# Fused causal attention and soft MoE: the sums of the last 128 queries added by VectorE, and a start without round trips for two pairs

## The chip, the cores and the metric

The kernel runs on 1 core of one Trainium2 chip. The metric is the device time of one execution in microseconds. The profile records one execution; its span is a little shorter than its time, and every row quoted below counts from the span's start.

## What is computed

Eight batches of eight heads, 576 tokens, head size 64. Each head has a causal attention whose scores get a bias from running sums `cum` of `max(s, 0)`; the output of all heads of a batch goes through a soft mixture of experts.

```python
scores = scale * np.matmul(q, k.transpose(0, 1, 3, 2))
s_pos = np.maximum(s, 0.0)
cum = np.cumsum(s_pos, axis=-1)
bias = -(cum[:, :, :, None] - cum[:, :, None, :])
scores = np.where(causal, -1000000000.0, scores + np.minimum(bias, 0.0))
scores = scores - np.max(scores, axis=-1, keepdims=True)
attn = np.exp(scores)
attn = attn / (np.sum(attn, axis=-1, keepdims=True) + 1e-09)
attn_out = np.matmul(attn, v)
...
logits = x @ phi
d = softmax(logits, axis=0)
slot_input = d.T @ x
slot_out[e] = np.maximum(slot_input[e] @ w1[e], 0.0) @ w2[e]
out = softmax(logits, axis=1) @ slot_out
```

## The kernel before

Two heads make a **pair** and lie in the two halves of the partitions; there are 32 pairs, four to a batch. For the pair p the kernel works in two passes over the scores.

The first pass finds the maximum of every query's row. `mxp` (L370) makes the scores with the queries in the partitions, in four groups `mx.p.0` to `mx.p.3`; groups 0 and 1 are the last 128 queries against keys 0 to 287 and 288 to 575, groups 2 and 3 the other queries. For each piece TensorE does a matmul of queries and keys (`w`) and a second one that adds the key's running sum: its stationary operand `ones2` holds ones in every 32nd row, its moving operand `g` the sums, split into a high and a low fp32r part. VectorE takes the maxima in `red` (L381): for group 0 a plain reduction (L389), for the others a custom operation (L392) that also adds the causal `mask` and is followed by a read of its accumulator.

Then the maxima go into the row form that the second pass needs: `f0` splits them on GpSimd (L403, L404), `f1` transposes them on TensorE (`mt`, L411), `f2` copies them on ScalarE (`hl`, L417), and `md` sends them by a DMA into rows of `g` (L424, L427). The sums come into other rows of `g` by the DMA `cum` (L357, L360). The second pass `sc` (L436) makes the scores again with the keys in the partitions, as three products of high and low parts plus one product from `g` that adds sum and maximum; ScalarE exponentiates (`ex`, L456), GpSimd cuts the causal corner (`cut`, L463) and adds up for the denominators (`zs`, L484 to L490), TensorE multiplies with v (`y`, L533).

A string `ORDER` lists all steps (`mx.16.0`, `f0.16`, `cut.15.0`, ...) and each engine executes its own in that order; SyncE issues nearly all DMAs from one queue. `busy.n` are n matmuls whose results nobody reads. The four expert weight arrays come in 64 blocks of 512 KB: some go early into `pre` (NPRE blocks), the rest into buffers that the attention no longer needs (`get`), the last ones into blocks that the first expert layer has read. The end of the program (from `sit`, L847) is the two expert layers and the output.

```python
groups = [[(0, 4, 0, 288)], [(0, 4, 288, 576)], [(0, 3, 0, 448), (448, 0, 0, 64)],
          [(0, 2, 0, 320), (320, 1, 0, 192)]]
for l, t, k in ((w[:, q0 - 128:q0], w, WK), (ones2, gt, KO)):
    for a, r in enumerate(half):
        nc.tensor.matmul(ps[a][:, d:d + hi - lo], l[r], t[r, k + lo:k + hi],
                         start=t is w, stop=t is gt)
```

## Time and profile before

| what | value |
|---|---|
| median of 3 runs | 415.88 us (414.97 to 416.27) |
| the profiled execution's time | 415.59 us |
| its span | 413.9 us |
| TensorE (PE) busy | 395.3 us, 96% |
| VectorE (DVE) busy | 284.0 us, 69% |
| GpSimd (POOL) busy | 274.8 us, 66% |
| ScalarE (ACT) busy | 239.6 us, 58% |

The profiled execution took 0.29 us less than the median. A share of the whole span mixes three stages: a start of some 21 us, the pairs until about 345 us, and the experts with the output. Each has its own limit, so the views are read by stage.

### The profile page before, as it was taken

The page shows a single profiled execution, that of the slowest core. Times are in us where ns is not written, and L with a number is a line of the kernel's source. Part 1 is how long each engine was busy: PE and PEld are TensorE (multiplying, and loading weights), DVE is VectorE, ACT ScalarE, POOL GpSimd, SP SyncE. Part 2 cuts the span into 40 slices and gives each one's busy share as a digit, 9 for nine tenths or more (in the row PEclk, how much of TensorE's full clock was granted, in tenths as well). Part 3 has the DMA queues.
Part 4 walks back from the last instruction along what each step waited for, and adds up shares of the span by engine and source line. Part 5 has one row for each costly group of instructions (what it writes and reads, how often), then busy time and mean ns, then how long its engine had stood idle before and what let it go on. Part 6 is the DMA issues. An engine that isn't in the chain of part 4 may idle for free.

```text
span 413.9 us, 14533 instructions
## 1 busy us (share of the span) xinstructions
PE 395.3 (96%) x5699; PEld 295.3 (71%) x5699; DVE 284.0 (69%) x952; ACT 239.6 (58%) x717; POOL 274.8 (66%) x376
## 2 busy tenths in 40 slices
PE   8999999999999999999999999999999999999950
PEld 8778777777787777777777787778777777435540
DVE  8956887877877787778767877787778547212460
ACT  3156766586768665866586768666865663220350
POOL 7069899888878888888788878887888740000000
PEclk9999999999999999999999999999999999999995
DMA  3424578526754475447644754463236789999998
GB/s 130 133 80 140 181 260 261 171 89 202 231 172 144 146 232 172 141 148 216 188 142 144 229 176 144 146 193 110 92 89 191 250 234 401 390 412 384 306 329 295
DMA packets 35252, 83.76 MB, mean 202 GB/s; under 512 B 4976, under 2 KB 14192, under 8 KB 35184
## 3 DMA queue, kind: packets, MB, share of 16 engines
q1 hardware_dynamic: 35168, 82.83, 60.6%
q8 instruction: 45, 0.74, 0.7%
q14 instruction: 23, 0.19, 0.1%
q10 hardware_dynamic: 16, 0.01, 0.0%
HBM read 72.43 MB, written 10.03 MB: 199 GB/s over the span
## 4 chain that ended last, share of the span: by engine, by line
PE 81%; DMA 4%; DVE 3%; ACT 2%; issue 2%; SPq 0%; DVEq 0%
PE s L445 25%; PE y L533 19%; PE mx L378 11%; PE sum L562 4%; PE m L1023 3%; PE m L995 3%; DMA g<-hl 3%; PE nat L601 3%; PE lt L666 2%; PE sl L786 2%; PE mt L411 1%; PE po L1061 1%; ACT arena L456 1%; PE x L522 1%; DVE arena L392 1%
## 5 line engine op out<-in xcount | busy, mean ns | idle before, releaser
L456 ACT ACTIVATE arena<-s 128x288 f32<-128x288 f32 (+4 forms) x384 | 114.9, 407 | 31.7 <-PE s L445 30.6
L445 PE MATMUL s<-w 64*128 64x288 f32 (+4 forms) x1152 | 109.2, 304 | 0.3 <-DVE nmin L743 0.2
L533 PE MATMUL y<-arena 128*64 128x512 f32 (+4 forms) x640 | 90.8, 427 | 0.0
L445 PEld LDWEIGHTS s<-w 64*128 64x128 f32 (+1 forms) x1152 | 81.9, 177 | 10.2 <-ACT arena L456 1.2
L463 POOL TENSOR_SCALAR_AFFINE_SELECT arena<-arena 128x256 f32<-128x256 f32 (+1 forms) x160 | 63.7, 411 | 23.6 <-ACT arena L456 22.0
L484 POOL TENSOR_TENSOR arena<-arena 128x896 f32<-128x896 f32 x31 | 69.3, 2237 | 8.7 <-PE mt L411 5.9
L533 PEld LDWEIGHTS y<-arena 128*64 128x64 f32 x640 | 42.5, 137 | 44.8 <-issue 34.1
L392 DVE CUSTOM_DVE_ANT_0 arena<-mx,arena 128x448 bf16<-128x448 f32 (+3 forms) x128 | 59.0, 461 | 17.6 <-PE mx L378 15.8
L378 PE MATMUL mx<-w 64*128 64x288 f32 (+4 forms) x384 | 56.6, 302 | 0.9 <-ACT w L341 0.9
L445 PE MATMUL s<-g 64*128 64x288 f32 (+4 forms) x384 | 56.5, 291 | 0.5 <-DMA g<-hl 0.5
L392 DVE CUSTOM_DVE_ANT_0 junk<-mx,arena 64x64 bf16<-64x64 f32 (+3 forms) x128 | 49.2, 385 | 10.4 <-PE mx L378 8.7
L378 PE MATMUL mx<-g,ones 64*128 64x288 f32 (+4 forms) x384 | 53.1, 300 | 0.0
L347 DVE TENSOR_TENSOR w<-arena,w 128x576 fp32r<-128x576 f32 x64 | 50.6, 810 | 0.2
L486 POOL TENSOR_TENSOR arena<-arena 128x640 f32<-128x640 f32 x31 | 48.3, 1557 | 2.4
L341 ACT CAST w<-arena 128x576 fp32r<-128x576 f32 x64 | 40.4, 677 | 13.7 <-DMA arena<-in_qk_dram 12.7
L545 ACT COPY arena<-y 128x512 f32<-128x512 f32 x32 | 18.8, 589 | 48.8 <-PE y L533 48.8
L389 DVE TENSOR_REDUCE mx<-mx 128x1 f32<-128x288 f32 x64 | 26.7, 447 | 27.5 <-PE mx L378 23.3
L378 PEld LDWEIGHTS mx<-w 64*128 64x128 f32 x384 | 38.5, 185 | 3.2 <-ACT w L341 1.0
L378 PEld LDWEIGHTS mx<-g,ones 64*128 64x128 f32 x384 | 38.2, 185 | 0.3
L445 PEld LDWEIGHTS s<-g 64*128 64x128 f32 (+1 forms) x384 | 35.1, 177 | 1.5 <-DMA g<-hl 1.0
L488 POOL TENSOR_TENSOR arena<-arena 128x384 f32<-128x384 f32 x31 | 31.8, 1026 | 2.4
L403 POOL TENSOR_SCALAR mh<-mx 128x10 fp32r<-128x10 f32 x32 | 20.1, 627 | 17.5 <-DVE mx L392 17.1
(168 smaller groups left out, 573.6 us busy)
## 6 DMA issues: line engine op xcount, KB each, us to landing
arena<-in_qk_dram SPq DMA_DIRECT2D x32, 576.0 KB
pre<-in_w_dram SPq DMA_DIRECT2D x36, 512.0 KB
arena<-in_v_dram SPq DMA_DIRECT2D x32, 320.0 KB
arena<-in_w_dram SPq DMA_DIRECT2D x19, 512.0 KB
arena<-rs SPq DMA_DIRECT2D x60, 144.0 KB
out_dram<-pre SPq DMA_DIRECT2D x20, 256.0 KB
ww<-in_w_dram SPq DMA_DIRECT2D x6, 512.0 KB
out_dram<-ww SPq DMA_DIRECT2D x8, 256.0 KB
```

Of the source, the lines that this page charges most:

```text
L341: nc.scalar.copy(w[:, o:o + S], st["raw", p][:, i, :])
L347: nc.vector.tensor_tensor(w[:, o + 2 * S:o + 3 * S], st["raw", p][:, i, :], w[:, o:o + S].bitcast(F32), op=ALU.subtract)
L378: nc.tensor.matmul(ps[a][:, d:d + hi - lo], l[r], t[r, k + lo:k + hi], start=t is w, stop=t is gt)
L389: nc.vector.tensor_reduce(m[:, a, c:c + 1], ps[:, d:d + w], axis=AX.X, op=ALU.max)
L392: nc.vector.tensor_tensor_reduce(out=junk()[r, 0:w], in0=ps[r, d:d + w], in1=mask[r, o:o + w], scale=1.0, scalar=m[:, a, 4:5] if i == 1 el ...
L445: nc.tensor.matmul(ps[a][0:n, d:d + hi - lo], t[r, ko + 128 * j:ko + 128 * j + n], t[r, qo + lo:qo + hi], start=x == 0, stop=x == 3)
L456: nc.scalar.activation(st["p", p][0:n, a, o + lo:o + hi], ps[0:n, d:d + hi - lo], AF.Exp, bias=0.0, scale=0.125)
L463: nc.gpsimd.affine_select(d, d, pattern=[[0, 2], [1, n]], compare_op=ALU.is_ge, fill=0.0, base=0, channel_multiplier=-1)
L484: eng.tensor_tensor(z[:, :, 128:576], pt[:, :, 128:576], pt[:, :, 576:1024], op=ALU.add)
L486: eng.tensor_tensor(z[:, :, 256:576], z[:, :, 256:576], pt[:, :, 1024:1344], op=ALU.add)
L488: eng.tensor_tensor(z[:, :, 384:576], z[:, :, 384:576], pt[:, :, 1344:1536], op=ALU.add)
L533: nc.tensor.matmul(y[r, lo - 64:512], vt[:, j, r], st["p", p][:, g, OFF[j] + lo - 128 * j:OFF[j] + 576 - 128 * j], start=(j == 0), stop=(j ...
```

## The change

For the pairs from 2 on, groups 0 and 1 lose the second matmul. In its place a DMA `cb` sends the pair's running sums (576 KB) from a new DRAM copy `cumf` to all 128 partitions, GpSimd's `cm` sets the causal corner of that tile to a large negative number, and VectorE's custom operation adds the tile while it searches the maximum. Two such tiles take 2304 words of each partition, and NPRE goes from 24 to 21.

For the pairs 0 and 1 the sums are added on TensorE straight from the fp32 tile `cum`, with a column of the identity as stationary operand; their maxima get into rows of `g` by 20 matmuls with a mostly zero operand `turn` and two copies on ScalarE, with no DMA. Their `low` parts move from VectorE to GpSimd, and some clearing of buffers moves from the start into a step `clear` on GpSimd after `f0.0`. Of the 46 `busy` matmuls of the start 9 are left. The sums now lie in partitions 0 to 31 and 64 to 95.

```diff
-NPRE = 24
+NPRE = 21
...
-    nc.sync.dma_start(out=s_sb, in_=s)
+    nc.sync.dma_start(out=s_sb[0:NP], in_=s[0:NP])
+    nc.scalar.dma_start(out=s_sb[64:64 + NP], in_=s[NP:NH])
...
+    op(("clear",), clear)
+    op(("ch", 0), lambda: nc.scalar.copy(cumhl[:, 0, :].bitcast(F32R), cum))
+    op(("ch", 1), lambda: nc.gpsimd.tensor_tensor(cumhl[:, 1, :].bitcast(F32R), cum, cumhl[:, 0, :], op=ALU.subtract), [("ch", 0)])
...
-            nc.vector.tensor_tensor(w[:, o + 2 * S:o + 3 * S], st["raw", p][:, i, :],
+            (nc.gpsimd if p < 2 else nc.vector).tensor_tensor(w[:, o + 2 * S:o + 3 * S], st["raw", p][:, i, :],
...
-                for l, t, k in ((w[:, q0 - 128:q0], w, WK), (ones2, gt, KO)):
+                for l, t, k in ((w[:, q0 - 128:q0], w, WK), (ones2, gt, KO) if p > 1 else (None, cum, 0))[:1 if p > 1 and c == 4 else 2]:
...
-                        nc.tensor.matmul(ps[a][:, d:d + hi - lo], l[r], t[r, k + lo:k + hi],
-                                         start=t is w, stop=t is gt)
+                        x = ident[r, 64 * a + p:64 * a + p + 1].broadcast_to([64, 128]) if l is None else l[r]
+                        nc.tensor.matmul(ps[a][:, d:d + hi - lo], x, t[r, k + lo:k + hi],
+                                         start=t is w, stop=t is not w or p > 1 and c == 4)
...
+                if c == 4 and p > 1:
+                    nc.vector.tensor_tensor_reduce(
+                        out=junk()[:, 0:w], in0=ps[:, d:d + w], in1=reg("cb", p % 2).rearrange("p (a x) -> p a x", a=2)[:, a, lo:hi], scale=1.0,
+                        scalar=m[:, a, 4:5] if i else NEG, op0=ALU.add, op1=ALU.max, accum_out=m[:, a, 4:5])
+                    continue
...
+        def cb():
+            nc.sync.dma_start(out=reg("cb", p % 2), in_=cumf[p:p + 1].broadcast_to([128, 2 * S]))
+
+        def cm():
+            d = reg("cb", p % 2).rearrange("p (a x) -> p a x", a=2)[:, :, S - 128:S]
+            nc.gpsimd.affine_select(d, d, pattern=[[0, 2], [-1, 128]], compare_op=ALU.is_ge, fill=NEG,
+                                    base=0, channel_multiplier=1)
...
+                for c in range(NCH):
+                    for k in range(4):
+                        nc.tensor.matmul(st["mt", p][c // 4][32 * k:32 * k + 32, 128 * (c % 4):128 * (c % 4) + 128],
+                                         turn[:, c, k, :], ident, start=True, stop=True)
...
+                nc.scalar.copy(gt[:, 0:512], st["mt", p][0])
...
+                nc.scalar.copy(gt[:, 512:KO], st["mt", p][1][:, 0:KO - 512])
...
-    op(("cw",), lambda: nc.sync.dma_start(out=cumd, in_=cumhl), [("cum", 1)])
+    def copy_full():
+        for a in range(2):
+            nc.sync.dma_start(out=cumf[:, S * a:S * a + S], in_=cum[64 * a:64 * a + NP])
```

`ORDER` is written anew as a whole. On TensorE in the middle of the program, at the start of pair 16's first pass (`mx_16`; `w` are its keys and queries, `g` and `ones` the sums), these rows stood before:

```order
L445 MATMUL s_1_0_3042<-g_96 128x288
L445 MATMUL s_1_1_3043<-g_96 128x288
L378 MATMUL mx_16_0_3065<-w_101 128x288
L378 MATMUL mx_16_1_3066<-w_101 128x288
L378 MATMUL mx_16_0_3065<-g_98,ones_109 128x288
L378 MATMUL mx_16_1_3066<-g_98,ones_109 128x288
L666 MATMUL lt_3072<-arena 32x128 x4
```

and these now:

```order
L493 MATMUL s_1_0_3057<-g_99 128x288
L493 MATMUL s_1_1_3058<-g_99 128x288
L398 MATMUL mx_16_0_3080<-w_104 128x288
L398 MATMUL mx_16_1_3081<-w_104 128x288
L714 MATMUL lt_3088<-arena 32x128 x4
```

The two matmuls with the sums are gone, and what surrounds them kept its order.

On GpSimd at the same place the last additions for pair 13's denominators (L490, now L538), the split `mh` of pair 15's maxima, and the cuts of pair 14 stood so before:

```order
L490 TENSOR_TENSOR arena<-arena 64x2x64
L403 TENSOR_SCALAR mh_3024<-mx_115 128x2x5
L404 TENSOR_TENSOR mh_3024<-mx_115,mh_3024 128x2x5
L463 AFFINE_SELECT arena<-arena 128x2x128 x3
L463 AFFINE_SELECT arena<-arena 64x2x64
```

and now, with `cm` of pair 16 as L430:

```order
L538 TENSOR_TENSOR arena<-arena 64x2x64
L444 TENSOR_SCALAR mh_3052<-mx_119 128x2x5
L445 TENSOR_TENSOR mh_3052<-mx_119,mh_3052 128x2x5
L430 AFFINE_SELECT arena<-arena 128x2x128
L511 AFFINE_SELECT arena<-arena 128x2x128 x3
L511 AFFINE_SELECT arena<-arena 64x2x64
```

`cm` stands behind the split and ahead of the next pair's cuts here; for the pairs 17 and 18 it stands ahead of the split.

On SyncE's DMA queue where a batch ends, from the DMA `md` of pair 13 (first L424 row) to that of pair 14, with the reciprocal denominators `rs` sent to all partitions, weights (`pre`), v and the next queries and keys between them, it was:

```order
L424 DMA g_98<-hl_2740 4x5x128
L357 DMA g_97<-cumd 4x576
L571 DMA arena<-rs_0_2724 64x576 x4
L860 DMA pre<-in_w_dram 128x1024
L506 DMA arena<-in_v_dram 128x640
L331 DMA arena<-in_qk_dram 128x1152
L571 DMA arena<-rs_0_2724 64x576 x2
L424 DMA g_96<-hl_2916 4x5x128
```

and it is now:

```order
L476 DMA g_101<-hl_2755 4x5x128
L426 DMA arena<-cumf 128x1152
L376 DMA g_100<-cumd 4x1x576
L619 DMA arena<-rs_0_2738 64x576 x4
L908 DMA pre<-in_w_dram 128x1024
L554 DMA arena<-in_v_dram 128x640
L350 DMA arena<-in_qk_dram 128x1152
L619 DMA arena<-rs_0_2738 64x576 x2
L476 DMA g_99<-hl_2931 4x5x128
```

One more transfer of 576 KB, `cb` (L426), has come in ahead of all that stands between the two.

## Rows read from the trace of the kernel before

**Rows 1.** The page, busy time of each engine: us, share of span, instructions.
```profile
PE 395.3 (96%) x5699; PEld 295.3 (71%) x5699; DVE 284.0 (69%) x952; ACT 239.6 (58%) x717; POOL 274.8 (66%) x376
```
**Rows 2.** Busy time in stretches: us, PE PEld DVE ACT POOL, PEclk, DMA share, GB/s.
```profile
280.00:320.00 40.00, 40.00 (x617) 31.27 (x614) 30.57 (x107) 26.33 (x83) 33.34 (x45) 1.00 0.38 119
360.00:380.00 20.00, 19.82 (x249) 8.86 (x241) 3.55 (x6) 2.39 (x4) 0.00 (x0) 1.00 1.03 410
```
**Rows 3.** Timeline of PE, first pass of pair 0: start us, us, what.
```profile
10.88 0.29 PE L378 MATMUL mx<-g,ones 64*128 64x288 f32 x2
11.02 0.29 PE L378 MATMUL mx<-w 64*128 64x288 f32 x2
11.15 0.30 PE L378 MATMUL mx<-g,ones 64*128 64x288 f32 x2
11.29 0.36 PE L378 MATMUL mx<-w 64*128 64x448 f32 x2
```
**Rows 4.** Chain of waits, in order: start us, us; matmuls sl end a batch.
```profile
100.35 0.86 PE sl L786 x8
...
141.43 0.86 PE sl L786 x8
...
152.00 6.41 DMA g<-hl
...
182.97 0.86 PE sl L786 x8
...
193.54 6.54 DMA g<-hl
...
224.63 0.86 PE sl L786 x8
```
**Rows 5.** Timeline of DVE, first maxima of pair 0.
```profile
11.25 0.82 DVE L389 TENSOR_REDUCE mx<-mx 128x1 f32<-128x288 f32 x2 [0.56 <-PE mx L378]
11.99 0.51 DVE L392 CUSTOM_DVE_ANT_0 arena<-mx,arena,mx 128x288 bf16<-128x288 f32 x1
12.42 0.08 DVE L392 DVE_READ_ACCUMULATOR2_ANT mx<- 128x1 f32 x1
```
**Rows 6.** Groups by line: busy us, mean ns | idle before, releaser.
```profile
L463 POOL TENSOR_SCALAR_AFFINE_SELECT arena<-arena 128x256 f32<-128x256 f32 (+1 forms) x160 | 63.7, 411 | 23.6 <-ACT arena L456 22.0
L488 POOL TENSOR_TENSOR arena<-arena 128x384 f32<-128x384 f32 x31 | 31.8, 1026 | 2.4
L562 PE MATMUL sum<-arena,onesl 128*32 128x72 f32 x1024 | 22.5, 228 | 0.0
```
**Rows 7.** Timeline of POOL and of PE around the split of a pair's maxima.
```profile
149.10 0.54 POOL L404 TENSOR_TENSOR mh<-mx,mh 128x10 fp32r<-128x10 f32 x1
...
151.41 0.28 PE L411 MATMUL mt<-ident,mh 128*20 128x128 f32 x1
```
**Rows 8.** Busy time in stretches of a batch's end, columns as in Rows 2.
```profile
144.00:146.00 2.00, 2.00 (x18) 1.14 (x18) 1.97 (x10) 1.43 (x3) 1.54 (x2) 1.00 0.09 24
...
154.00:156.00 2.00, 2.00 (x14) 1.00 (x14) 1.94 (x11) 1.43 (x3) 1.92 (x3) 1.00 0.91 222
```
**Rows 9.** Timeline of the start: casts, scan, first matmul, filler, split, first scores.
```profile
4.50 1.67 DVE L268 TENSOR_TENSOR_SCAN arena<-arena 64x576 f32<-64x576 f32 x1
5.38 1.25 ACT L341 CAST w<-arena 128x576 fp32r<-128x576 f32 x2 [3.31 <-DMA arena<-in_qk_dram]
10.64 0.40 PE L378 MATMUL mx<-w 64*128 64x288 f32 x2
13.45 2.27 PE L937 MATMUL busy<-ident 128*128 128x128 f32 x18
16.49 0.20 POOL L404 TENSOR_TENSOR mh<-mx,mh 128x10 fp32r<-128x10 f32 x1
21.22 0.68 PE L445 MATMUL s<-w 64*128 64x288 f32 x6
```
**Rows 10.** Timeline of SyncE's queue at the end: first output transfers.
```profile
383.09 15.54 SPq L1067 DMA_DIRECT2D out_dram<-pre  x20
```

More of the change, by code (lines that the diff above doesn't have):

```diff
@@ new lines @@
+e1.7.1.0 ex.31.2.1 cut.31.0 ex.31.3.0 get.11 a.30.1 cut.31.3 zc.31 cut.31.2 a.30.2 z.31.0 ax.31 a.30.3 a.30.4 rb.30
+ev.30 get.14 z.31.1 get.15 evx.31 t6.6 get.13 a.31.0 nr.29 z.31.2 a.31.1 z.31.3 nr.28 sm.31 a.31.2 e1.7.2.0 a.31.3
+nr.30 a.31.4 rb.31 ev.31 get.16 get.18 get.17 lt.28 nr.31 lt.29 lt.30 get.22 lt.31 get.20 t7.6 c0.7 t2.7 t3.7 busy.1
+m.0 nat.31 t8.6 nat.28 m.1 nat.29 natd.31 natd.28 m.2 natd.29 nat.30 m.3 t4.7 nat0.7 m.4 natd.30 c1.7 get.23 natd0.7
+t5.7 m.5 get.24 t6.7 busy.2 m.6 t7.7 m.7 s0.7 s1.7 ct t8.7 get.28 get.21 get.19 get.12 sit.0 get.26 get.27 get.25
@@ L164 @@
+sit.1 s2.7 s2p.7
 """
@@ L316, in every32, with clear @@
         return t.bitcast(F32).rearrange("(a r) x -> a r x", r=32)[:, i, :]
+    def clear():
+        for t in gs[2:]:
+            nc.gpsimd.memset(t[:, KO:].bitcast(F32), -1.0)
+            ones_rows(t)
+        nc.gpsimd.memset(onesl, 0.0)
+        nc.gpsimd.memset(onesl[:, 4 * HP - 1:4 * HP], 1.0)
+        nc.gpsimd.memset(dn[64:128, 1, :], 0.0)
+        nc.gpsimd.memset(reg("x", 0)[64:128, 0:DM], 0.0)
+        for i in range(NPB):
+            nc.gpsimd.memset(reg("p", i).rearrange("p (a x) -> p a x", a=2)[64:128, :, 1536:1600], 0.0)
+        nc.gpsimd.memset(acc, 0.0)
+    op(("clear",), clear)
+    op(("ch", 0), lambda: nc.scalar.copy(cumhl[:, 0, :].bitcast(F32R), cum))
+    op(("ch", 1), lambda: nc.gpsimd.tensor_tensor(cumhl[:, 1, :].bitcast(F32R), cum, cumhl[:, 0, :], op=ALU.subtract), [("ch", 0)])
     def scores(p):
@@ L408, in f1 @@
         def f1():
+            if p < 2:
+                st["mt", p] = [bank(f"mt{i}") for i in range(2)]
+                for c in range(NCH):
+                    for k in range(4):
+                        nc.tensor.matmul(st["mt", p][c // 4][32 * k:32 * k + 32, 128 * (c % 4):128 * (c % 4) + 128],
+                                         turn[:, c, k, :], ident, start=True, stop=True)
+                return
             mh = st.pop(("mh", p))
@@ L421, in md @@
         def md():
-            hl = st.pop(("hl", p))
-            if p:
-                nc.sync.dma_start(out=every32(gt, 1)[:, 0:KO].rearrange("l (c q) -> l c q", c=NCH), in_=hl.bitcast(F32))
+            if p < 2:
+                nc.scalar.copy(gt[:, 512:KO], st["mt", p][1][:, 0:KO - 512])
                 return
-            for a in range(2):
-                (nc.scalar if a and p == 0 else nc.sync).dma_start(out=every32(gt, 1)[2 * a:2 * a + 2, 0:KO].rearrange("l (c q) -> l c q", c=NCH),
-                                  in_=hl[2 * NCH * a:2 * NCH * (a + 1)].bitcast(F32))
+            nc.sync.dma_start(out=every32(gt, 1)[:, 0:KO].rearrange("l (c q) -> l c q", c=NCH), in_=st.pop(("hl", p)).bitcast(F32))
         op(("md", p), md, [("f2", p)])
@@ L492, in scores @@
         g = old(NZ)
-        op(("zc", p), zc, [("cut", p, 0), dep("sm", g)])
+        op(("zc", p), zc, [("cut", p, 0), dep("sm", g), ("clear",) if p == 0 else None])
         for i in range(4):
@@ L874, in tile_attn_softmoe, with copy_cum @@
     op(("cst",), (fetch, g4, cst[:, 0:128]), [("load", 3)])
-    op(("cw",), lambda: nc.sync.dma_start(out=cumd, in_=cumhl), [("cum", 1)])
+    def copy_cum():
+        for a in range(2):
+            nc.sync.dma_start(out=cumd[a], in_=cumhl[64 * a:64 * a + NP])
+    def copy_full():
+        for a in range(2):
+            nc.sync.dma_start(out=cumf[:, S * a:S * a + S], in_=cum[64 * a:64 * a + NP])
+    op(("cf",), copy_full, [("ch", 0)])
+    op(("cw",), copy_cum, [("cum", 1)])
     op(("phi",), load_phi, [("load", 2)])
@@ L924, in tile_attn_softmoe @@
         op(("pre", i), (get, pre[:, 1024 * i:1024 * (i + 1)]), [("load", min(4 + i, NP - 1))])
[L925 removed]
+    room.sort(key=lambda r: max([0 if x[0] in ("low", "red") else 1 if x[0] == "s" else 3 if x[0] == "t7" else 2 for x in r[1]]))
     last = None
```

353 lines of the change are left out of this document (180 added, 173 removed).

## The prediction

> **What bounds the kernel now.** I read the page's busy times first, then the stretches, the timeline of TensorE, the chain of waits, and last the start and the end. TensorE is busy 96% of the span, far ahead of DVE, POOL and ACT [rows 1]. A busy record alone doesn't show that an engine is at its limit, because matmuls overlap; so see two more things. In the stretch from 280 to 320 us TensorE has no idle time at all, while POOL has 33.3 and DVE 30.6 of 40 us [rows 2]. And a pair of 288-column matmuls (one for each head) starts 0.13 to 0.14 us after the one ahead of it, though its record lasts 0.29 [rows 3]: 288 columns in 0.135 us are 2.1 columns a nanosecond, near the upper of the clock's two levels, and the granted clock of the stretch is 1.00. So in the middle of the program time goes as TensorE's columns go. The chain of waits repeats itself with 41.08 us for a batch of four pairs (100.35 to 141.43). Two batches take 41.54 and 41.66, and in each of them the chain holds a DMA `g<-hl`, the `md`, for 6.4 to 6.5 us [rows 4]: where a batch ends, the queue is so full that the maxima arrive about half a microsecond late. That is the weak place of this kernel.
>
> **The sums of the last queries, pairs 2 to 31.** Each pair loses two steps of 288 columns (both heads run side by side), so 2 x 0.135 = 0.27 us of TensorE, and 30 x 0.27 = **8.1 us**. This lies on the path that sets the end wherever TensorE has no idle time.
>
> On DVE two plain reductions (0.82 us for both) become two custom operations, which follow each other at 0.43 us with the accumulator's read inside [rows 5]: 30 x 0.04 us, hidden, as DVE has 9 us of idle time in 40 [rows 2]. The operand is now fp32 and not bf16. No row shows this form; a custom operation of 288 columns already goes at some 0.67 columns a nanosecond, and if the wider operand doubled its time, the four of a pair would cost 1.7 us more, still under the 2.3 us that DVE idles for each pair. I take nothing.
>
> On POOL `cm` is one more corner cut of 128 x 256 elements, 0.41 us [rows 6], 1.6 us in a batch: 33.3 becomes about 35.9 of 40 us (the same work in a shorter stretch, plus 1.6). That is close. Where it would bite is the split of the maxima: at a batch's end POOL ends it at 149.64 and TensorE transposes at 151.41 [rows 7], so 1.77 us are left, against 0.41 for `cm` and 0.27 for the earlier TensorE. I take nothing for it; behind it the cuts come late next.
>
> **The transfer of the sums.** `cb` brings 0.59 MB a pair. At the rate of the weight loads, 410 GB/s, it takes 1.4 us of the DMA engines; at that of the stretch in which the `rs` rows go to all partitions, 222 GB/s at a share of 0.91, it takes 2.4 us [rows 2, 8]. Nearest is the latter, since this is such a transfer too. In most pairs it falls into idle queues (a share of 0.38 from 280 to 320). At a batch's end it stands ahead of the four and two `rs` transfers, weights, v, queries and keys that are ahead of `md`. Some of it fills the gap before (a share of 0.09 from 144 to 146), the rest makes `md` later. Lower bound: nothing, if it all goes into that gap. Upper bound: 2.4 us at each of the seven batch ends, 16.8 us. I take half a microsecond, which is what a late `md` costs in the two batches that show one, at five of the seven, an estimate that leaves two ends the room that most of them have now: **+2.5 us**. Bounds of the range: 0 and 7 (1 us at all seven).
>
> **The start.** Before, the first matmul waits for the sums' round trip and starts at 10.64, though the casts end at 6.63 and the scan at 6.17 [rows 9]; now it may start at 6.7. From there the first scores start, before, at 21.22, held by the `md` of pair 0. DVE took some 4.8 us for pair 0's maxima (from 11.25 [rows 5] to just ahead of the split, whose second half is at 16.49); with two reductions of pair 1 now between them, 0.8, and a first matmul's results at about 7.5 it is done at 13.1. POOL has five operations of 576 elements ahead of the split, which by 1.03 us for 384 take 1.5 each [rows 6]: 7.7 us from the casts' end, 14.3. Then come the split (0.5, two rows like that at 16.49), 20 matmuls of 128 columns, and two ScalarE copies of 640 columns together (0.7 by the casts). By the `sum` matmuls, which take 32 columns of the array too, 22.5 us for 32 pairs of 16 x 72 columns, the 2560 columns take 1.6 us [rows 6]; by the filler, 0.25 us each (two records to a matmul), 5 us [rows 9]. The former is the nearer shape. That gives 14.3 + 0.5 + 1.6 + 0.7 = 17.1, and with 0.9 for the handovers between four engines (an estimate) 18.0: 3.2 us earlier. TensorE has then about 0.7 us less of pairs 1 and 2 done than before at 21.22, by the five steps of rows 3's kind that it lacks. The fp32 sums of the two pairs cost 1600 columns each at 0.25 us for 128, 3.1 us a pair; that lies beside the waits for DVE and POOL, where 46 filler matmuls ran. If they ran longer than those waits, they would be what is late next. I take **-2.5 us**, with the bounds -4 and +1 (`clear` stands on POOL between the two splits and may delay pair 1).
>
> **The end.** With NPRE down by 3 and 2304 more words of buffers (two blocks of 1024), one block less can be loaded before the experts, and one more is refilled among them. The DMA engines are full from 360 to 380 (share 1.03) [rows 2], and the output starts at 383.09 behind them [rows 10]. A block is 0.52 MB, 1.3 us at 410 GB/s; between 0 and 1.3 I take **+0.7 us**.
>
> **The sum.** -8.1 + 2.5 - 2.5 + 0.7 = -7.4 us, against the profiled execution's 415.59: **408.2 us**, 1.8% below the median of 415.88. A measurement of this kernel tells 0.3%, 1.25 us, from no change.
>
> **The rivals.** *Everything hides.* `cb` fits into idle queues, and the start gains its bound: 415.6 - 8.1 - 4 = 403.5. For it: 38% share in the quiet stretch. Against: the chain already shows `md` late twice.
>
> *The batch ends give it back.* `md` comes 1.3 us later at all seven: 415.6 - 8.1 - 2.5 + 9.1 + 0.7 = 414.8, no change that can be told.
>
> *Slower.* The same mechanism at its upper bound: `cb` pushes the whole 2.4 us in front of `md` at seven batch ends, +16.8: 422.5. It decides from 1.6 us a batch end on, where the waits eat 8.1 + 2.5 - 0.7 and 1.25 more. Against it: the gap at 144 to 146.
>
> *TensorE is not what bounds.* Then the columns removed buy nothing between 40 and 340 us, and 415.6 - 2.5 + 2.5 + 0.7 = 416.3 remains, no change. The pitch in rows 3 speaks against it. The Trainium skill (Perfetto Trace Analysis, Identifying the Most-Contended Engine) has a rule for this rival: matmul busy time says little about how near TensorE is to its limit, and the busy share of the weight loads says more. By that rule the 71% of PEld [rows 1] leave room, and the time would be this rival's 416.3; the trace answers with start-to-start times and not with busy time, so I give the rule's case little.
>
> **How the numbers follow.** The forecast has 0.65, everything hides 0.17, batch ends give it back 0.07, slower 0.07, TensorE not the bound 0.04. The first two are faster by over 0.3%: 0.82; the third and last are within it: 0.11; slower 0.07. The range runs from 403.0, just under the second case, to 413.6, where the forecast's terms stand at +7 for the batch ends and -1 for the start (415.6 - 8.1 - 1 + 7 = 413.5); what is left out is 0.18.
>
> **What would show it.** Right: no `g,ones` matmuls for groups 0 and 1, and a batch of four pairs in the chain at about 40.0 us, 40.5 where `md` is late; first scores near 18 us; POOL near 36 of 40 us, without TensorE waiting for its cuts or splits. Wrong: TensorE idle at scores for `g<-hl` by over a microsecond in each batch, VectorE's first maxima waiting for `cm` or for `cb`, a batch still at 41 us, or the outputs starting later after the last pair than before.

## The result, and the profile after

The changed kernel takes 420.57 us (median of 20 runs, 415.09 to 439.84) against 416.0 for the kernel before (median of 20). The ratio over the runs that nothing disturbed is 1.0068, interval [1.0047, 1.0089]: slower by 0.7%, where the forecast was 408.2 us, 1.8% faster. The profiled execution took 415.09 us (span 413.4) and is the fastest of the 20, so its profile shows little of the loss: its span is even 0.5 us shorter than that of the kernel before. The second profile, of `again` below, is of a run of 415.33 us. The 4 to 5 us that a typical run takes longer stand in neither; what they are due to follows from the times of the experiments alone.

The engines and the main DMA queue on the page of the changed kernel:

```profile
PE 387.8 (94%) x5607; PEld 284.2 (69%) x5607; DVE 288.6 (70%) x1006; ACT 242.5 (59%) x722; POOL 288.2 (70%) x413
...
q1 hardware_dynamic: 39480, 100.59, 71.8%
```

TensorE is busy 7.5 us less than in [rows 1], and the span is only 0.5 us shorter. The queue's packets fill 71.8% of 16 engines' span; before they filled 60.6%, with 82.83 MB. The difference, 71.8% of 413.4 less 60.6% of 413.9, is 46.0 us for 30 `cb`: 1.53 us of all 16 engines for each.

The chain of waits of the changed kernel, the lines that answer to [rows 4] (start us, us, what; `sl` ends a batch):

```profile
68.02 5.00 DMA g<-hl
...
102.96 0.99 PE sl L834 x8
...
143.24 0.86 PE sl L834 x8
...
183.38 0.86 PE sl L834 x8
...
223.53 0.86 PE sl L834 x8
...
265.22 3.56 DMA rs<-sr
268.84 4.35 DMA arena<-rs
...
305.33 0.86 PE sl L834 x8
...
311.12 5.68 DMA arena<-rs
...
347.10 0.86 PE sl L834 x8
```

Put beside the chain of before; the first four rows are points in time (scores and transposes from TensorE's timelines), the others durations:

| stage | before | after | difference |
|---|---|---|---|
| first scores start | 21.22 | 16.80 | -4.4 |
| transpose of pair 6's maxima | 69.14 | 67.17 | -2.0 |
| transpose of pair 8's maxima | 90.61 | 93.11 | +2.5 |
| `sl` of the first batch | 100.35 | 102.96 | +2.6 |
| three batches from there | 124.28 | 120.57 | -3.7 |
| two batches from there | 82.16 | 81.80 | -0.4 |
| one batch from there | 40.51 | 41.77 | +1.3 |
| from there to the span's end | 66.6 | 66.3 | -0.3 |

So the loop's gain is there: 40.14 us for a batch that nothing holds up, against 41.08. Of the 3.7 us that three batches gain, 1.0 comes from the two late `md` of [rows 4], which did not come back in this execution. The start's gain is there at 16.80 and half gone by pair 6. Then the first batch end takes 4.5 us, and with two late ends, at 274 and 316 us, the last three batches take 0.9 us more than before instead of less.

The first batch end, in stretches of the changed kernel (columns as in [rows 2]):

```profile
70.00:72.00 2.00, 0.80 (x15) 0.56 (x8) 1.46 (x5) 0.41 (x1) 0.81 (x3) 1.00 0.86 227
72.00:74.00 2.00, 0.93 (x14) 0.91 (x16) 0.17 (x1) 0.07 (x1) 1.13 (x2) 1.00 1.01 398
74.00:76.00 2.00, 2.00 (x18) 1.83 (x16) 1.44 (x6) 1.57 (x5) 1.35 (x1) 0.60 1.04 221
76.00:78.00 2.00, 2.00 (x16) 1.45 (x12) 0.30 (x4) 1.42 (x3) 1.50 (x5) 0.55 1.01 237
```

TensorE is idle for 2.3 of the 4 us from 70 to 74, waiting for the `md` that was issued at 68.02 behind four `rs` transfers and a `cb`:

```profile
73.07 0.40 PE L493 MATMUL s<-g 64*128 64x288 f32 x2 [2.27 <-DMA g<-hl]
```

In the 4 us after that the granted clock is 0.60 and 0.55, near the lower of its two levels (1.2 GHz), while the DMA share is above 1.0.

The two late losses are something else. Timelines of TensorE, VectorE and GpSimd in the changed kernel, at 273 to 278 us:

```profile
277.75 0.66 PE L649 MATMUL nat<-ident,arena 128*128 128x128 f32 x4 [0.74 <-DVE mx L417]
```
```profile
273.29 0.88 DVE L641 TENSOR_TENSOR arena<-arena 128x576 f32<-128x576 f32 x1 [1.48 <-DMA arena<-rs]
...
274.84 2.17 DVE L641 TENSOR_TENSOR arena<-arena 128x576 f32<-128x576 f32 x1
```
```profile
274.29 2.10 POOL L532 TENSOR_TENSOR arena<-arena 128x896 f32<-128x896 f32 x1
```

`nr` (L641, u times the reciprocal denominators) waits 1.48 us for its `rs` row. The next `nr` then starts half a microsecond into GpSimd's large addition and takes 2.17 us instead of 0.75; it ends 0.6 us after the addition does. The maxima behind it on VectorE are late, and `nat` (the transposes of `nr`'s results, on TensorE) waits until they have been read. At 316.90 the same follows an addition that began at 315.71.

### The profile page after: what moved, and what is told of

It reads as the page before. It is cut to its first block, busy times and chain, and to the rows that moved or that the text cites. A ratio compares the mean times of both kernels' runs of the same rounds, so it can differ in the third digit from the quotient of the medians.

```text
span 413.4 us, 14563 instructions
## 1 busy us (share of the span) xinstructions
PE 387.8 (94%) x5607; PEld 284.2 (69%) x5607; DVE 288.6 (70%) x1006; ACT 242.5 (59%) x722; POOL 288.2 (70%) x413
## 3 DMA queue, kind: packets, MB, share of 16 engines
q1 hardware_dynamic: 39480, 100.59, 71.8%
## 4 chain that ended last, share of the span: by engine, by line
PE 74%; DMA 9%; POOL 4%; DVE 4%; issue 3%; SPq 2%; ACT 1%; DVEq 0%; POOLq 0%
PE s L493 23%; PE y L581 17%; PE mx L398 8%; PE sum L610 4%; PE nat L649 3%; PE m L1078 3%; PE m L1050 3%; DMA arena<-cumf 3%; DMA arena<-rs 2%; PE lt L714 2%; PE sl L834 2%; PE po L1116 1%; PE mt L459 1%; DMA g<-hl 1%; DMA arena<-in_v_dram 1%
## 5 line engine op out<-in xcount | busy, mean ns | idle before, releaser
L581 PE MATMUL y<-arena 128*64 128x512 f32 (+4 forms) x640 | 93.3, 428 | 0.4 <-DMA arena<-in_v_dram 0.4
L493 PEld LDWEIGHTS s<-w 64*128 64x128 f32 (+1 forms) x1152 | 84.1, 178 | 10.8 <-issue 1.9
L532 POOL TENSOR_TENSOR arena<-arena 128x896 f32<-128x896 f32 x31 | 66.3, 2138 | 6.8 <-PE sum L610 4.5
L417 DVE CUSTOM_DVE_ANT_0 arena<-mx,arena 128x320 bf16<-128x320 f32 (+3 forms) x128 | 58.6, 458 | 17.8 <-PE mx L398 16.2
L493 PE MATMUL s<-g 64*128 64x288 f32 (+4 forms) x384 | 58.6, 293 | 2.3 <-DMA g<-hl 2.3
L417 DVE CUSTOM_DVE_ANT_0 junk<-mx,arena 128x192 bf16<-128x192 f32 (+3 forms) x128 | 49.5, 387 | 8.8 <-PE mx L398 7.0
L641 DVE TENSOR_TENSOR arena<-arena 128x576 f32<-128x576 f32 x30 | 26.4, 884 | 8.8 <-DMA arena<-rs 8.7
L398 PE MATMUL mx<-g,ones 64*128 64x448 f32 (+1 forms) x240 | 31.1, 303 | 0.0
L430 POOL TENSOR_SCALAR_AFFINE_SELECT arena<-arena 128x256 f32<-128x256 f32 x30 | 15.1, 502 | 16.2 <-DMA arena<-cumf 15.5
L398 PEld LDWEIGHTS mx<-g,ones 64*128 64x128 f32 x240 | 23.6, 185 | 0.4
```

What stands on the lines that cost most here:

```text
L398: nc.tensor.matmul(ps[a][:, d:d + hi - lo], x, t[r, k + lo:k + hi], start=t is w, stop=t is not w or p > 1 and c == 4)
L417: nc.vector.tensor_tensor_reduce(out=junk()[r, 0:w], in0=ps[r, d:d + w], in1=mask[r, o:o + w], scale=1.0, scalar=m[:, a, 4:5] if i == 1 el ...
L493: nc.tensor.matmul(ps[a][0:n, d:d + hi - lo], t[r, ko + 128 * j:ko + 128 * j + n], t[r, qo + lo:qo + hi], start=x == 0, stop=x == 3)
L532: eng.tensor_tensor(z[:, :, 128:576], pt[:, :, 128:576], pt[:, :, 576:1024], op=ALU.add)
L581: nc.tensor.matmul(y[r, lo - 64:512], vt[:, j, r], st["p", p][:, g, OFF[j] + lo - 128 * j:OFF[j] + 576 - 128 * j], start=(j == 0), stop=(j ...
L641: nc.vector.tensor_tensor(u, u, st.pop(("r", p)), op=ALU.mult)
```

## The experiments

Each is the changed kernel with one edit, where nothing else is said. "Ratio" is to the kernel before, measured beside the run, with its interval.

| run | median us | ratio |
|---|---|---|
| again | 419.27 | 1.0059 [1.003, 1.0089] |
| cb_thin | 412.94 | 0.9922 [0.9889, 0.9956] |
| thin_no_cm | 413.81 | 0.9939 [0.9914, 0.9965] |
| loop_as_before | 415.63 | 0.9995 [0.9971, 1.0018] |
| cb_early | 424.22 | 1.0172 [1.0127, 1.0217] |
| first_end | 420.77 | 1.012 [1.0082, 1.0157] |
| nr_late | 425.91 | 1.0239 [1.0212, 1.0265] |
| both_moves | 425.96 | 1.0223 [1.0198, 1.0248] |
| cb_act | 427.38 | 1.0183 [1.014, 1.0227] |
| pre_early | 418.86 | 1.0042 [1.0004, 1.008] |
| z_split | 423.47 | 1.0166 [1.0117, 1.0216] |
| hybrid | 413.87 | 0.9951 [0.9924, 0.9978] |
| hybrid_pre | 415.95 | 0.9986 [0.9957, 1.0014] |
| hybrid3 | 416.65 | 0.9988 [0.996, 1.0017] |
| hybrid0 | 416.51 | 0.9994 [0.9967, 1.0021] |
| hybrid_late | 413.12 | 0.992 [0.9898, 0.9943] |
| hybrid_first | 412.88 | 0.993 [0.99, 0.9961] |

### What the parts are worth

**again**: no edit. Expected:

> The changed kernel once more, for a second profile: its 20 runs lie between 415 and 440 us and the profiled one is the fastest of them, so one profile may not show what the others lose. Theory A (the DMA queue of the first batch end and of some later ones is too full with `cb` in it, TensorE then runs dry, and its clock falls): 417 to 421 us, with idle time of TensorE between 58 and 80 us, a stretch at a granted clock of about 0.6 behind it, and more or longer waits for `rs`, v or `g<-hl` than the first profile has. Rival B (the loop itself is slower, by POOL or DVE): the batches in the middle of the program take over 40.6 us each instead of the 40.15 of the first profile, with no low clock needed.

Its profile has the idle time at the first batch end too (1.45 us before scores for `g<-hl`, then 2.04 us before a product with v whose transfer took 8.0 us), and 1.46 us at 277.77 as above, and its batches in between take 40.14 to 40.18 us. Rival B falls. The granted clock stayed at 1.00 here, and yet pair 6 to pair 8 took 25.75 us, against 25.94 in the first profile and 21.47 before. So the low clock comes and goes and is not the cause of this loss.

**cb_thin**:

```diff
-            nc.sync.dma_start(out=reg("cb", p % 2), in_=cumf[p:p + 1].broadcast_to([128, 2 * S]))
+            n = 2 * S if p < 4 else 64
+            nc.sync.dma_start(out=reg("cb", p % 2)[:, 0:n], in_=cumf[p:p + 1, 0:n].broadcast_to([128, n]))
```

> The `cb` transfers of the pairs 4 to 31 carry 64 columns instead of 1152 (32 KB instead of 576 KB); every instruction stays, so DVE adds sums of an earlier pair. Left out: the right sums of the last 128 queries of those pairs. Theory A: what the change loses, it loses to these bytes; 8.1 us of TensorE columns and some 2.5 us of the start come through, 405 to 409 us, and no low clock. Theory A2 (what loses is the new order of the first batch, v and weights late and bunched, whatever `cb` weighs): the first batch end keeps its idle time and its low clock, 412 to 416 us. Rival B (POOL's `cm` or DVE): no change from the changed kernel, 417 to 420 us.

Beside it the changed kernel took 419.27: the bytes of `cb` cost 6.3 us (5.7 by the two ratios). But 412.9 is not 408. The profile is again of the fastest run, 410.51 us. It has no wait for `md` left; it does have three others of TensorE above a microsecond, two behind VectorE's maxima and one without a releaser:

```profile
74.47 0.63 PE L650 MATMUL nat<-ident,arena 128*128 128x128 f32 x4 [1.58 <-DVE mx L417]
...
273.48 0.66 PE L650 MATMUL nat<-ident,arena 128*128 128x128 f32 x4 [1.13 <-DVE mx L417]
...
323.57 0.28 PE L460 MATMUL mt<-ident,mh 128*20 128x128 f32 x1 [1.21 <-issue]
```

The one at 273.48 stands behind this pair, VectorE's and GpSimd's rows of `cb_thin`:

```profile
270.20 2.54 DVE L642 TENSOR_TENSOR arena<-arena 128x576 f32<-128x576 f32 x1
```
```profile
270.01 2.11 POOL L533 TENSOR_TENSOR arena<-arena 128x896 f32<-128x896 f32 x1
```

**thin_no_cm**: `cb_thin`, and `cm` returns without an instruction for p > 3.

> The run with thin `cb` (412.9 us), and `cm` left out as well for the pairs 4 to 31 (the corner keeps what the first mask left). If GpSimd's 0.41 us a pair is part of what that run still lacks to the forecast of 408.2, as the splits on GpSimd that TensorE waits for suggest, 410 to 411.5 us and no wait of TensorE for GpSimd's split; if it is hidden, as the forecast has it, 412.3 to 413.5 us.

No gain that can be told: GpSimd's masking itself is hidden in the loop. What the run can't show is a `cm` that waits for a full `cb`, since its transfers are thin. Its profile, of a run of 415.78 us, has `md` late although the bytes are gone: TensorE waits 0.87 us for `g<-hl` at 156.22 and 1.26 at 321.35. So the missing wait of `cb_thin` belongs to that one execution.

**loop_as_before**: both matmuls for groups 0 and 1 of all pairs again, the maxima by the old operations, `cb` and `cm` out of `ORDER`.

> The changed kernel with the loop of the kernel before: for the pairs 2 to 31 the sums of the last queries come from TensorE again, no `cb`, no `cm`; the new start and the new order stay. Theory A: the start's gain alone, 412 to 414.5 us against 416.0 of the kernel before, and no low clock at the first batch end. Theory A2 (the new order of the first batch is what loses): the first batch end stays bad and TensorE has 8 us more to do, 417 to 422 us. Rival B says nothing else than A here.

The new start and the new order together are worth nothing that can be measured, 415.63 against 415.89. And `cb_thin`, which differs from this run by the matmuls that are gone (and by VectorE's sums, `cm` and a thin `cb`), is only 2.7 us faster (3.0 by the ratios), where the forecast has 8.1.

### Which bytes, where, and in whose queue

**cb_early**:

```diff
-... red.14.3.0 cb.15 cast.15.1 ...
+... red.13.1.1 cb.15 evx.11 ...
```

and likewise for the pairs 11, 19, 23, 27 and 31.

> In the changed kernel the `cb` of the pairs 11, 15, 19, 23, 27 and 31, which stands between the batch end's `rs` write and the transfers of `rs` to all partitions, is moved ahead of them, right behind the last maxima of the pair two before (one pair earlier, into a stretch with a DMA share below 0.5). The first batch is untouched. Theory A: the waits of `nr` for `rs` at the ends of batches 1 to 6 go, some 1 to 3 us: 415 to 417.5 us where the changed kernel takes 418 to 419, and what is left is the first batch. Theory A2 and rival B: within 0.5 us of the changed kernel.

Slower by 5 us. The transfer moved from ahead of `rs` to ahead of `load.16` and `md.13` (for pair 15), and TensorE now waits 2.98 us for `g<-hl` at 100.88, 1.42 at 166.23 and 1.87 at 280.99. Where it stood was the better place.

**first_end**: `load_v.4` and `load_v.5` earlier, `pre.0` behind `md.3`, `pre.1` behind `md.4`, `cb.8` behind `red.6.1.1`.

> Only the order of DMAs before and at the first batch end differs from the changed kernel: v of the pairs 4 and 5 one step earlier, two weight blocks into the quiet stretch from 35 to 55 us, and the `cb` of pair 8 from between the `rs` transfers and `md` to ahead of them, into the time in which the `rs` write is under way. Theory 1 (what the changed kernel loses at its first batch end, 4.5 us between the pairs 6 and 8, is this queue: `md` and v late, TensorE idle, its clock low): the wait for `g<-hl` at 70 to 73 us goes, no low clock, 414 to 416.5 us where the changed kernel takes 419. Rival (the first batch end loses its time to the sheer bytes, in whatever order): the wait moves to another transfer, 418 to 420 us.

The wait at 73 us went and no low clock was left, but the first batch still ended at 102.61. The waits turned up as 1.89 us behind the maxima at 74.18, 1.21 us for `g<-hl` at 97.97, and at the ends of the batches 2 and 3, where nothing was edited, `md` came late (7.67 and 6.36 us in the chain). Theory 1 in its simple form falls.

**nr_late**: at the ends of the batches 2 to 6 `nr.(4b+1)`, its `nat` and the `rd` behind it stand behind all maxima of the pair.

> In the changed kernel, at the ends of the batches 2 to 6, VectorE's second `nr` (u times reciprocal denominators, both from SBUF) and its `nat` and `rd` behind it move from between the maxima of the pair to behind all of them. Theory 2 (an `nr` that starts while GpSimd adds 128x896 elements stands still until that addition ends, 2.2 to 2.5 us instead of 0.75, and the maxima behind it are late; `cb` makes the `rs` rows late enough for that at some batch ends): the idle time of TensorE in front of `nat` at 270 to 280 and 315 to 320 us goes, 2 to 3 us less than the changed kernel, 416 to 417.5 us, and the batches there take 40.2 instead of 41.8 us. Rival (there the maxima are late because `rs` is late, whatever GpSimd does): the waits move to the `nr` behind or to `nat`, 418 to 420 us.

**both_moves**: the two edits together.

> Both moves together. If theories 1 and 2 both hold, their gains add: 411 to 414 us, faster than the kernel before (416) and near the kernel whose `cb` carries almost nothing (412.9), with batches of 40.2 us throughout. If only one holds, 414 to 417.5 us.

Both are slower than the changed kernel by some 6 us. In `nr_late` the waits for `nat` at 281.78 and 330.21 (0.78 and 1.51 us) are now put down to `nr` itself, and `g<-hl` came late at 160.81 and 203.10. Moving a late step moves the wait. From 80 us on no `nr` of this profile takes over 1.2 us, so the long ones went, and with them went no time: that they cost the changed kernel what it loses at its late ends is not shown by this run.

**cb_act**:

```diff
-            nc.sync.dma_start(out=reg("cb", p % 2), in_=cumf[p:p + 1]...
+            (nc.scalar if p > 3 else nc.sync).dma_start(out=reg("cb", p % 2), in_=cumf[p:p + 1]...
```

> The changed kernel, with the `cb` transfers of the pairs 4 to 31 issued by ScalarE into its own DMA queue instead of SyncE's, at the same places of the order. Theory 1a (what hurts is that `md` and `rs` stand behind `cb` in one queue): they land earlier, 413 to 416 us. Theory 1b (the 16 engines are full of bytes, whoever queued them): `g<-hl` and `rs` are as late as before, and ScalarE pays some 0.3 us for each issue and for its waits: 418 to 423 us.

Another queue does not help; it costs another 1.2%. How much of that is ScalarE's own part, 0.33 us for the issue of a `cb` at 205.10 and its waits, was not separated. The Trainium skill (DMA: Bandwidth & Descriptors, Issuing engines are not separate DMA queues) says that the transfers of all engines run on the same 16 DMA engines; this run, with 1.018 against 1.006, fits that and does not prove it.

**pre_early**: seven weight blocks from the batch ends to 31 to 55 us.

> In the changed kernel seven of the 21 weight blocks (0.52 MB each), the two at the first batch end and the five between the `rs` transfers of the later ones, are loaded between 31 and 55 us instead, where the DMA share is 0.45. Theory 1b: 0.52 MB less in each batch end is nearly the 0.59 MB of a `cb`: 414 to 417 us, and the waits for `g<-hl` and `rs` get shorter. Rival (what counts is not the bytes of the batch end but the handover from `rs` to `nr`, or VectorE and GpSimd in each other's way): 418 to 421 us.

**z_split**:

```diff
-                eng.tensor_tensor(z[:, :, 128:576], pt[:, :, 128:576], pt[:, :, 576:1024], op=ALU.add)
+                for a in range(2):
+                    eng.tensor_tensor(z[:, a, 128:576], pt[:, a, 128:576], pt[:, a, 576:1024], op=ALU.add)
```

> In the changed kernel GpSimd's addition of 128x896 elements (2.1 us) becomes two of 448, one for each head; GpSimd gets some 0.15 us more work a pair. Theory 2 (an `nr` stands still while such an addition runs): no `nr` takes over 1.9 us any more, where rows of 2.2 to 2.7 us exist now, and the waits of TensorE for `nat` behind late maxima shrink by half: 417 to 419 us, 1 to 2 us less than the changed kernel. Rival (the long `nr` has another cause, the DMA writes into its rows for example): rows of over 2 us stay, and the time is that of the changed kernel or, by GpSimd's additional work, up to 2 us more.

`pre_early` lies at the changed kernel's time: all its batches from 147 to 268 us take 40.14, and it loses at 56 us (2.02 us idle, at a DMA share of 0.94 from 55 to 60 us), where the early blocks now crowd, what it wins later. `z_split` failed: an `nr` at 237.49 took 3.23 us, through both halves (237.51, 2.25 us for the two), the cut behind them (239.72, 0.40) and into the next addition (240.20). As a remedy the split is wrong; as a test it did not decide.

### Fewer bytes at the batch ends

**hybrid**:

```diff
+        send = p > 1 and not (p >= 7 and p % 4 in (3, 0))
...
-                for l, t, k in ((w[:, q0 - 128:q0], w, WK), (ones2, gt, KO) if p > 1 else (None, cum, 0))[:1 if p > 1 and c == 4 else 2]:
+                for l, t, k in ((w[:, q0 - 128:q0], w, WK), (ones2, gt, KO) if p > 1 else (None, cum, 0))[:1 if send and c == 4 else 2]:
```

and `send` in the other three places, `cb` and `cm` of those pairs out of `ORDER`.

> In the changed kernel the pairs 7, 8, 11, 12, ... 27, 28, 31, whose `cb` stands around the `rs` transfers of a batch end, get the sums of their last queries from TensorE as before, with no `cb` and no `cm`; 17 of the 30 pairs keep the change. Theory 1b (at a batch end the 16 DMA engines have no room for these bytes, in whatever order or queue they come): the waits for `g<-hl` and `rs` at the batch ends fall back to what the kernel before has, and 17 pairs keep some 0.24 us each: 411 to 414 us where the changed kernel takes 419 to 420 and the kernel before 416. Rival (the new order and the start lose the time, or VectorE and GpSimd do): 415.5 to 419 us, near the run with the loop as before, 415.6.

**hybrid_pre**: `hybrid` and `pre_early` together.

> `hybrid` and `pre_early` together: 1.1 MB less in each batch end. Theory 1b: at least as good as `hybrid`, 410 to 413 us, no wait for `g<-hl` over 0.3 us in any batch. Rival: as `hybrid`, within 0.7 us.

13 pairs gave their gain up, and the kernel became 5.4 us faster than the changed one (4.5 by the ratios). `hybrid_pre` ends its first batch at 104.77, 4.4 us after the kernel before, and then has five batches in a row of 40.4 to 40.5 us.

**hybrid3** and **hybrid0**: `p % 4 in (3,)` and `p % 4 in (0,)`.

> In the changed kernel only the pairs 7, 11, ... 31 go back to sums from TensorE, those whose `cb` stands ahead of the `rs` transfers of a batch end; 23 pairs keep the change. If it is this place that costs (the bytes ahead of `rs` and of `md`), most of the 5.4 us between the changed kernel and `hybrid` come back while 6 more pairs than in `hybrid` keep 0.24 us: 412.5 to 414 us. If it is the `cb` behind the `rs` transfers that costs, 417 to 419 us.

> The opposite half: only the pairs 8, 12, ... 28 go back to TensorE, those whose `cb` stands behind the first `rs` transfers; 24 pairs keep the change. If the place ahead of `rs` costs, 416.5 to 419 us; if the place behind costs, 412.5 to 414.5 us. If both runs lie near 416, the cost goes with the bytes in the batch end and not with one place.

Both at about 416.6, half way between the changed kernel and `hybrid`: neither place alone is the culprit, and each half of the bytes is worth about half.

**hybrid_late**: `hybrid`, with `pre.8`, `pre.12` and `pre.16` behind the `load_v` one pair later, and `pre.20` behind `md.27`.

> `hybrid`, with four of the five weight blocks that stand between the `rs` transfers of batch ends moved one pair later, where in `hybrid` no `cb` goes; nothing is moved into the start. In the run with early weights and without those `cb` all batches took 40.5 us and no wait was left after 105 us. Theory 1b: the same here without that run's loss in the first 105 us: 411 to 413.5 us, batches of 40.5 us. Rival: as `hybrid`, 413.2 to 414.5 us.

0.8% faster than the kernel before. The chain of `hybrid_late`, its batches:

```profile
141.78 0.86 PE sl L835 x8
...
182.32 0.86 PE sl L835 x8
...
222.86 0.86 PE sl L835 x8
...
263.39 0.86 PE sl L835 x8
...
303.94 0.86 PE sl L835 x8
```

Four batches in a row take 40.54 us: two of the four pairs keep the change, which is 0.54 us under 41.08, and none of these batch ends takes it back. The batch ahead of them takes 41.16 us, the last one about a microsecond more than 40.5: at 131.83 GpSimd has waited 3.11 us for a `cb`, and at 321.14 `md` is late again, by 0.50 us.

**hybrid_first**: `hybrid_late`, with `pre.0` where `cb.7` stood, `pre.1` a pair later, and `load_v.4` and `load_v.5` one step earlier.

> `hybrid_late`, and at the first batch end the two weight blocks taken out as well (one to where the `cb` of pair 7 stood, one a pair later) and v of the pairs 4 and 5 requested one step earlier. If what the start gains is lost at the first batch end to the crowd of transfers there, 411 to 412.5 us and the first `sl` at 98 to 99.5 us instead of 100.6; if it is lost to `nr` standing still beside GpSimd's additions there (1.8 us three times in `hybrid_late`), within 0.7 us of `hybrid_late`, 412.5 to 413.8.

412.88 us; the first batch ended at 100.04, not at 98 to 99.5. It cannot be told from `hybrid_late`. These two are the best versions found.

### VectorE beside GpSimd

**probe**: ahead of all steps

```diff
+        for i in range(4):
+            nc.gpsimd.tensor_tensor(x[:, 1792:2688], x[:, 0:896], x[:, 896:1792], op=ALU.add)
+        for i in range(16):
+            nc.vector.tensor_tensor(y[:, 0:576], y[:, 0:576], y[:, 576:1152], op=ALU.mult)
```

> The changed kernel with a measurement ahead of everything: after one clearing each, GpSimd does four additions of 128x896 elements one behind the other while VectorE does sixteen products of 128x576 (the shape of `nr`, both operands from SBUF), in rows that nothing else touches; the whole program starts later by that, so its time is not compared. Theory 2: a product that meets an addition takes over 1.2 us, up to 2.7 us, or the addition waits for it and takes over 2.4 us instead of 2.1; the products behind the last addition take 0.70 to 0.76 us. Rival (the long `nr` comes from transfers or from a late operand): all sixteen take 0.70 to 0.80 us and the additions 2.1 us.

All sixteen products in one line (duration ns, min/median/max), then single ones from VectorE's timeline and the additions from GpSimd's, whose other operations follow them until 28.9 us:

```profile
L344 DVE TENSOR_TENSOR arena<-arena x16: 757/1834/2512, 9.2 to 33.5; 128x576 f32<-128x576 f32 x16
```
```profile
9.22 0.76 DVE L344 TENSOR_TENSOR arena<-arena 128x576 f32<-128x576 f32 x1
...
10.02 2.51 DVE L344 TENSOR_TENSOR arena<-arena 128x576 f32<-128x576 f32 x1
...
30.33 3.93 DVE L344 TENSOR_TENSOR arena<-arena 128x576 f32<-128x576 f32 x5
```
```profile
9.84 2.07 POOL L342 TENSOR_TENSOR arena<-arena 128x896 f32<-128x896 f32 x1
...
11.99 2.47 POOL L342 TENSOR_TENSOR arena<-arena 128x896 f32<-128x896 f32 x1
```

The first product, beside no addition, takes 0.76 us. The second meets an addition and takes 2.51: the addition runs from 9.84 to 11.91, the product ends at 12.53. The next addition takes 2.47 instead of 2.07, since it waits for the product in its turn. The last five, with GpSimd done, take 0.79 each. The first half of theory 2 is shown: in the probe the two take turns, whole instruction by whole instruction, and no transfer has a part in it (the DMA share is 0.00 from 8 to 24 us). The other half, that `cb` brings `nr` to such a place and that this is what the changed kernel loses, is not shown by it. The Trainium skill (SBUF — State Buffer, SBUF: two separate sides) says that a VectorE operation with two SBUF inputs and a GpSimd operation that reads SBUF lock a shared pair of ports against each other, the loser blocked until the other ends; the trace agrees, with 0.76 against 2.51 us. The product of `z_split`, which was not served between two additions, is more than that sentence says.

## Why the prediction was wrong

The medians of four kernels that were measured beside each other split the miss, each difference uncertain by 1 to 2 us:

| step | forecast | measured |
|---|---|---|
| start, order and end (before to `loop_as_before`) | -1.8 | -0.3 |
| matmuls gone, hardly any bytes (`loop_as_before` to `cb_thin`) | -8.1 | -2.7 |
| the bytes of `cb` (`cb_thin` to `again`) | +2.5 | +6.3 |
| together | -7.4 | +3.4 |

Two steps failed above all: the gain of the matmuls was taken to stay whole, and the price of the transfer was too small. The split holds for this order of the steps.

**The sums of the last queries, -8.1.** The pace is right in kind and 1 us too large: an undisturbed batch went from 41.08 to 40.14 us, 0.235 us a pair and not 0.27, 7.1 us for 30 pairs. What failed is that all of it would stay on the path: of 7.1 us only 2.7 come through in `cb_thin`, in whose profile TensorE waits at three places for 3.9 us; how far that explains it stays open (below). In the undisturbed batches TensorE's work does set the time of the loop, and the rival "TensorE is not what bounds" falls, with the reading of the weight loads' share that stood for it.

**VectorE and `cm`, 0.** Right for the work itself: the custom operation with the fp32 operand takes 0.45 to 0.52 us, and leaving `cm` out gained nothing. Wrong where `cm` waits for a late `cb` and holds up the split of the maxima behind it. In the profiled execution GpSimd waits for `cb` 11 times, 15.5 us in all, and behind two of these waits in the loop TensorE waits for the split, by 0.56 us at 102.69 and 0.34 at 134.25. The chain of waits holds the first of the two, a `cb` that took 5.40 us from 95.66; GpSimd's and TensorE's rows:

```profile
101.18 0.41 POOL L430 TENSOR_SCALAR_AFFINE_SELECT arena<-arena 128x256 f32<-128x256 f32 x1 [0.84 <-DMA arena<-cumf]
```
```profile
102.69 0.28 PE L459 MATMUL mt<-ident,mh 128*20 128x128 f32 x1 [0.56 <-POOL mh L445]
```

At the start it is the same. GpSimd's timeline of the changed kernel there:

```profile
20.28 0.41 POOL L430 TENSOR_SCALAR_AFFINE_SELECT arena<-arena 128x256 f32<-128x256 f32 x1 [2.83 <-DMA arena<-cumf]
...
21.03 0.26 POOL L440 TENSOR_SCALAR arena<-mx 128x10 fp32r<-128x10 f32 x1
```

A `cm` of the loop's first pairs waits 2.83 us for a `cb` whose rows went through DRAM, and the split of pair 1's maxima stands behind it.

**The transfer, +2.5.** This step failed by its size, and its mechanism is only a part. It asked how late `md` would be at a batch end, took half a microsecond at five of seven, and the bounds 0 and 7. `cb_thin` measures 6.3 us, near the upper bound. In the two profiles of the changed kernel TensorE waits for `md` at one end only, the first, by 2.27 and 1.45 us. At the ends of the batches 2 to 4 in the profiled execution `cb` costs nothing, as the free stretch from 144 to 146 [rows 8] had promised. It costs at the first batch end, which the step did not look at by itself: there v, `rs`, weights and two `cb` fall together (DMA share 0.86 to 1.04 from 70 to 78 us), and TensorE is idle first and then has a low clock, 4.5 us between the pairs 6 and 8. Beside the way through `cm` (above) there is one more that the prediction did not have: `rs` comes late to `nr` (VectorE idles 8.8 us ahead of its 30 `nr`, before 1.8), `nr` runs into GpSimd's addition, and the maxima behind it are late. How the 6.3 us divide among these ways was not measured.

The prediction took VectorE and GpSimd as independent, and a row of the kernel before would have told otherwise. At its first batch end `nr` already met an addition, in VectorE's and GpSimd's timelines of before:

```profile
70.36 2.00 DVE L593 TENSOR_TENSOR arena<-arena 128x576 f32<-128x576 f32 x1 [0.86 <-DMA arena<-rs]
```
```profile
69.63 2.12 POOL L484 TENSOR_TENSOR arena<-arena 128x896 f32<-128x896 f32 x1
```

At the later ends `nr` came first: at 151.68 it took 0.75 us, 0.2 us ahead of the addition, which took 2.53. Such a meeting needs no `cb`: in `loop_as_before`, which has none for these pairs, the `nr` at 192.58 took 2.58 us.

**The start, -2.5.** TensorE's timeline of the changed kernel, first scores and the 20 matmuls for pair 1's maxima:

```profile
16.80 0.74 PE L493 MATMUL s<-w 64*128 64x320 f32 x6
...
21.34 1.59 PE L454 MATMUL mt<-ident,arena 128*32 128x128 f32 x40 [0.24 <-POOL arena L440]
```

The first scores came 4.4 us earlier than in [rows 9] here and 2.6 in `again` (18.64), around the 3.2 of the forecast. But `loop_as_before` shows no gain in the end. Two things were not in the sum: the 20 matmuls for pair 1 take 1.59 us on TensorE, where a transpose took 0.28, and pair 1's split came late (above). What is left is lost at the first batch end even without `cb`: in `loop_as_before` pair 6's transpose is still 1.7 us ahead of before, at 67.41, and the first batch ends at 100.35, as before. How much of that is the order and how much `nr` beside GpSimd (0.94 us idle at 74.80) was not separated.

**The end, +0.7.** From the last `sl` but one the rest took 66.3 us against 66.6: nothing lost. (The upper end of the range, worked out as 413.5, has no 0.7 in it; with it, it would be 414.2.)

**The rivals.** "The batch ends give it back" named the right resource and a time (414.8) near the fastest execution, but its mechanism, `md` late by 1.3 us at all seven ends, is not what the trace shows. "Slower", with a chance of 0.07, had the sign and the nearest time (422.5) by the same mechanism at twice the price. The profiles show neither: `md` is late at some ends only, and other steps beside it.

**Of the signs named:** no `g,ones` matmuls for groups 0 and 1, batches near 40.0 us and first scores near 18 us (16.80 and 18.64) all came true; GpSimd is busy 34.35 of the 40 us from 280 to 320, not 36, and TensorE does wait for its split. Of the signs against, GpSimd's waits for `cb` came true, though not VectorE's, and a wait for `g<-hl` above a microsecond came at one batch end, not at each.

**What stays open.** Why the waits appear at other batch ends from run to run: in `first_end` and `z_split` `md` was late at the ends of the batches 2 and 3, whose order was not edited, in `thin_no_cm` at ends where `cb` carries almost nothing, and before it was late at two. An arrival a few hundred nanoseconds earlier or later may be enough, but no run controls it. And why so little of the loop's gain comes through without the bytes: `cb_thin` lacks 7.2 us to what the forecast's other terms make, 405.7. Two of its three long waits stand behind VectorE's maxima; waits of that kind stand in `loop_as_before` too (0.94 us at 74.80, 1.00 at 195.90), so that part may belong to the new order and not to the change in the loop. What is behind the wait at 323.57 was not tried.

## What to carry to other kernels

Before adding a transfer, add up the bytes of the fullest stretch that it falls into, not of the average one, and give the first such stretch its own reading: here the 13 transfers of 0.59 MB (1.53 us of all DMA engines each) around the batch ends cost some 5 us more than they saved (`hybrid` against the changed kernel), and with the 17 others batches of 40.54 us came out. Where an exchange of engine time for DMA time pays in some places only, make it in those: 17 of 30 pairs, with the transfers of the crowded ends left out, beat both kernels (0.992). And before a step on VectorE is allowed to become later, look at what GpSimd does at the later time.
